# Changing sides between VectorE and GpSimd for 34 two-operand steps, with a new order for the first third

## The chip, the cores and the metric

The kernel runs on one core of a Trainium2 chip. The metric is the device time of one execution in microseconds; the median of three runs of the kernel before is 460.57 (460.49 to 461.0). TensorE (PE) does matrix products, VectorE (DVE) and GpSimd (POOL) do elementwise work, ScalarE (ACT) does activations and copies, SyncE (SP) issues nearly all transfers.

## The reference

A gated linear attention is followed by a two-layer network over its outputs:

```python
f = 1 / (1 + exp(-f_logit))                 # B=4, H=8, S=768, D=48
for t in range(S):
    state = f[:, :, t, :, None] * state + einsum('bhd,bhe->bhde', k[:, :, t], v[:, :, t])
    y[:, :, t] = einsum('bhd,bhde->bhe', q[:, :, t], state)
x = y.transpose(0, 2, 1, 3).reshape(3072, 384)
h = x @ w_in                                # 384 x 2048
out = (h * clip(h + 3, 0, 6) / 6) @ w_out   # 2048 x 384
```

## The kernel before

**Attention.** The sequence is cut into 24 units (4 batches x 6 chunks of 128 positions), numbered chunk by chunk. For unit i: `load`, `loadq`, `loadv` bring gates, q with k, and v (SP); `gate` (ScalarE, line 388) takes the sigmoid; `back` (VectorE scan, 395) makes suffix products, `rend` (411) their reciprocal, `fwd` (419) prefix products, `end` (ScalarE, 414) a copy of the chunk's whole decay. `kmul` (408) and `qmul` (424) multiply k and q by these, on VectorE or GpSimd. TensorE then does `tk` (transpose of k, 482), copied out by `ktok` (ScalarE, 489), `kv` (501), `att` (463), masked by `mask` (VectorE, 470), `qs` (533) and `av` (550); `carry0`, `carry1` (514 to 523) and `decay` (427) hand on the state. `xh`, `xl` (569, 580 or 582) split the result in a high and a low part, and `hole` copies rows within it by DMA; four units make a group of 512 tokens.

**Network.** Each fp32 product is done in three passes of fp32r (high x high, and the two mixed ones). For each of the 16 slices f of the hidden layer the weights come by `ld` and are converted once: `lim` (290 or 292), `z` (298), `mid` (305), `dif` (310), `top` (314) build the word, `high` (ScalarE, 326) the high part, `low` (329, or its halves `lowi`, `lowo`) the low part, on VectorE or GpSimd. For group g and slice f, token number 16g + f: `mm1` (619, nine matmuls), `relu` (ScalarE, 629), `g` (VectorE, 633, reads PSUM), `gh` (ScalarE, 642: high part), `gl` (646: low part, VectorE or GpSimd), `mm2` (669, nine matmuls, the last three of which read gl's result). The first slices of group 0 run in halves (`mm1a`, `relua`, `ga`, `mm2a`, and `...b`; 691 to 710).

**Order.** The program is one list, `ORDER` (line 55), of 1518 tokens `step.index[.banks]`; a loop (998 to 1033) emits them in that order, and each engine executes its own instructions in the list's order (1036 to 1040), waiting where an input or a buffer isn't ready. A step in `ON_POOL` (46) goes to GpSimd, otherwise to VectorE (line 353). SP's transfers stand in the same list, so one that must wait for a free buffer holds up those behind it. `load.i` waits for `qmul.i-2`, `loadq.i` for the last TensorE reader of unit i-3. `warm` and `tiny` are filler matmuls on zeros.

```python
    def engine(op, i):
        return nc.gpsimd if f"{op}.{i}" in ON_POOL else nc.vector
...
    for ins in nc.cur_bb.bb.instructions[begun:]:
        if ins.engine in ORDERED:
            if ins.engine in ordered:
                after(ins, ordered[ins.engine])
            ordered[ins.engine] = ins
```

Of the kernel before, what the change touches and what calls it, by code (L numbers as in the profile page):

```python
# [80 lines left out]
qmul.8 ktok.8 g.14 load.10 att.8.2 g.15 gh.14 kv.8.2 g.16 mm1.17.4 mask.8 rend.9 gl.14 fwd.9 mm2.14 gate.10 gh.15
qmul.9 gl.15 mm2.15 lowo.0 back.10 mm1.19.1 outs.0 outv.1 end.9 gh.16 outs.2 kmul.9 gl.16 relu.17 mm1.18.0 od.2
load.11 rend.10 relu.19 g.17 od.0 decay.8 carry0.8 fwd.10 mm2.16 relu.18 g.19 end.10 carry1.8 g.18 tk.9.3 qmul.10
load.12 mm1.20.4 loadv.10 ktok.9 od.1 gh.17 kmul.10 lowo.1 gh.18 gate.11 decay.9 gl.17 qs.8.0 att.9.2 loadq.11 av.8
kv.9.2 xh.8 carry0.9 mm2.17 gate.12 carry1.9 mask.9 decay.10 lowo.2 back.11 mm1.21.2 gl.18 end.11 gh.19 gl.19 xl.8
tk.10.3 relu.21 mm2.18 ktok.10 g.21 relu.20 rend.11 back.12 qs.9.0 gh.21 fwd.11 att.10.2 loadq.12 av.9 kv.10.0 qmul.11
mm2.19 g.20 load.13 loadv.11 carry0.10 gl.21 loadv.12 carry1.10 rend.12 mm1.22.4 fwd.12 mask.10 mm2.21 relu.22 g.22
kmul.12 decay.11 gh.22 kmul.11 mm1.23.3 gate.13 qmul.12 xh.9 back.13 load.14 hole.8 relu.23 gl.22 mm2.22 xl.9 g.23
hole.9 tk.11.4 qs.10.0 ktok.11 att.11.2 gh.20 loadq.13 av.10 gate.14 gl.20 kv.11.0 loadv.13 tk.12.4 rend.13 mm2.20
ktok.12 gh.23 end.12 gl.23 mask.11 mm1.24.4 decay.12 kmul.13 mm1.25.3 mm2.23 relu.25 relu.24 g.25 g.24 mm1.29.3 gh.24  # L90
gl.24 fwd.13 mm1.26.4 relu.29 gh.25 xh.10 qmul.13 gl.25 mm2.25 load.15 xl.10 relu.26 carry0.11 back.14 mm2.24 g.29
g.26 qs.11.0 gh.26 att.12.2 gl.26 av.11 kv.12.2 xh.11 loadv.14 mm2.26 hole.10 gh.29 carry1.11 mask.12 gate.15
carry0.12 loadq.14 carry1.12 rend.14 mm1.27.4 tk.13.2 relu.27 mm1.30.3 g.27 gl.29 xl.11 mm2.29 relu.30 hole.11 gh.27
g.30 end.13 kmul.14 mm1.28.1 gl.27 gh.30 ktok.13 gl.30 decay.13 back.15 tk.14.0 mm2.30 fwd.14 mm1.31.2 qmul.14 load.16
mm1.32.4 relu.31 relu.28 g.31 end.14 g.28 mm2.27 relu.32 ktok.14 qs.12.0 gh.28 att.13.2 gh.31 loadq.15 gl.28 av.12
g.32 kv.13.2 xh.12 mm2.28 decay.14 gate.16 mask.13 rend.15 carry0.13 carry1.13 fwd.15 mm1.33.4 xl.12 qs.13.2 qmul.15
gl.31 load.17 att.14.0 loadv.15 av.13 kv.14.0 xh.13 mm2.31 relu.33 xl.13 kmul.15 back.16 hole.13 tk.15.2 g.33 end.16
loadq.16 mm1.35.3 ktok.15 hole.12 carry0.14 outv.4 gh.32 end.15 outs.3 gl.32 loadv.16 gate.17 rend.16 mm1.36.2 gh.33
decay.15 fwd.16 outs.5 relu.35 mm2.32 g.35 carry1.14 qmul.16 gl.33 load.18 mm1.34.4 kmul.16 gh.35 back.17 mm2.33
relu.34 relu.36 g.34 g.36 tk.16.3 gl.35 gh.34 mm1.41.4 ktok.16 gl.34 mask.14 qs.14.2 att.15.0 loadq.17 av.14 od.5 od.3  # L100
od.4 kv.15.0 xh.14 mm2.35 xl.14 mask.15 carry0.15 rend.17 mm2.34 decay.16 fwd.17 gh.36 relu.41 g.41 qs.15.0 gh.41
att.16.2 qmul.17 gl.36 av.15 gl.41 kv.16.2 xh.15 mm2.36 gate.18 back.18 mm2.41 carry0.16 rend.18 xl.15 fwd.18 hole.15
mm1.38.4 carry1.16 loadv.17 mask.16 load.19 carry1.15 loadv.18 loadq.18 mm1.40.0 relu.38 mm1.37.3 relu.40 mm1.39.1
relu.37 g.37 g.38 qmul.18 load.20 mm1.44.3 kmul.17 hole.14 gh.38 g.40 gl.38 mm1.43.0 relu.39 gh.40 gl.40 mm2.38 g.39
relu.43 mm2.40 gh.37 end.18 gate.20 gl.37 g.43 mm1.42.1 kmul.18 gh.39 end.17 relu.44 gl.39 g.44 mm2.39 mm2.37 mm1.47.2
gh.44 gh.43 relu.42 gl.43 mm1.46.0 g.42 relu.47 gl.44 g.47 mm2.44 mm2.43 gh.42 gl.42 mm1.51.3 gh.47 relu.46 gl.47
back.20 mm1.45.2 g.46 tk.18.0 relu.45 mm2.42 ktok.18 g.45 relu.51 g.51 tk.17.4 gh.46 mm2.47 ktok.17 gl.46 gate.19
qs.16.0 gh.45 att.17.2 loadq.19 gl.45 av.16 kv.17.0 mask.17 mm2.46 xh.16 decay.18 decay.17 mm1.49.3 mm2.45 relu.49
g.49 carry0.17 xl.16 mm1.48.4 outs.6 back.19 outs.8 gh.51 od.8 od.6 qs.17.0 relu.48 att.18.2 loadq.20 g.48 av.17
# [1048 lines left out]
```

## Time and profile before

| what | us |
|---|---|
| median of three runs | 460.57 |
| profiled execution, first to last instruction | 458.9 |
| TensorE busy | 448.2 |
| VectorE busy | 329.8 |
| ScalarE busy | 225.9 |
| GpSimd busy | 95.0 |

The profile is one execution of the program. Its span goes from the first to the last instruction; a run's time is measured around it. "Busy" is the union of an engine's instructions; the ends of matmuls are modelled. In rows of the trace L408 is line 408 of the kernel, `out<-in` are the program's names for tiles, and `[0.31 <-POOL qkf L408]` says that the engine was idle for 0.31 us before this row and which instruction ended that. The pitch of a full-width matmul (512 columns) is 0.216 us.

### The profile page before, as it was taken

The numbers are of one execution on the slowest core, as the hardware profiler recorded it, in microseconds if no ns is written. First come the engines' busy times: TensorE is split into PE (matmuls) and PEld (weight loads), VectorE is DVE, ScalarE is ACT, GpSimd is POOL, SyncE is SP. The second block draws the span as 40 slices with busy tenths as digits, with TensorE's granted clock in tenths as the row PEclk, the third lists the DMA queues.
The fourth block names the chain that finished last, engine by engine and source line by source line (L and its number), as shares of the span: only waits on it lengthen the run. The fifth ranks groups of instructions, "written<-read, shape, count | busy, mean of one in ns | idle before, by whom it ended". The sixth has DMA issues, their size and how long they took to land.

```text
span 458.9 us, 11919 instructions
## 1 busy us (share of the span) xinstructions
PE 448.2 (98%) x5092; PEld 387.8 (85%) x5092; DVE 329.8 (72%) x538; ACT 225.9 (49%) x390; POOL 95.0 (21%) x110
## 2 busy tenths in 40 slices
...
GB/s 308 270 273 367 413 213 150 99 54 25 182 107 107 23 82 72 123 93 110 84 1 0 102 71 142 62 60 1 70 75 14 14 1 1 23 49 0 1 1 75
DMA packets 19116, 44.95 MB, mean 98 GB/s; under 512 B 2544, under 2 KB 8816, under 8 KB 19056
## 3 DMA queue, kind: packets, MB, share of 16 engines
...
q8 instruction: 42, 0.69, 0.6%
...
q14 instruction: 18, 0.15, 0.1%
...
## 4 chain that ended last, share of the span: by engine, by line
PE 90%; DMA 3%; DVE 3%; issue 1%; ACT 1%; SPq 1%; DVEq 0%; ACTq 0%
PE o L669 33%; PE pair L619 28%; PE single L619 11%; DMA raw<-w 3%; PE pair L533 3%; PE o L833 3%; PE pair L550 2%; PE pair L463 2%; PE single L833 2%; PE pair L833 2%; PE pair L501 2%; PE pair L482 1%; ACT workings L290 0%; DVE workings L314 0%; PE single L482 0%
## 5 line engine op out<-in xcount | busy, mean ns | idle before, releaser
L669 PE MATMUL o<-gg,weight 128*128 128x512 f32 x633 | 148.7, 382 | 0.3 <-issue 0.3
L619 PE MATMUL pair<-xts,weight 128*128 128x512 f32 x594 | 137.6, 381 | 0.0
L669 PEld LDWEIGHTS o<-gg,weight 128*128 128x128 f32 x633 | 117.6, 189 | 16.5 <-issue 0.2
L619 PEld LDWEIGHTS pair<-xts,weight 128*128 128x128 f32 x594 | 110.6, 189 | 15.5 <-DVE tg L633 0.3
L646 DVE TENSOR_TENSOR gg<-tg,gg 128x512 fp32r<-128x512 f32 x76 | 56.2, 746 | 34.4 <-ACT gg L642 34.0
L633 DVE SCALAR_TENSOR_TENSOR tg<-tg,pair 128x512 f32<-128x512 f32 x66 | 44.9, 682 | 41.3 <-ACT tg L629 40.9
L629 ACT ACTIVATE tg<-pair,half 128x512 f32<-128x512 f32 x66 | 44.9, 684 | 59.4 <-PE pair L619 56.7
L642 ACT ACTIVATE gg<-tg 128x512 fp32r<-128x512 f32 x79 | 48.8, 626 | 48.6 <-PE o L669 37.8
L619 PE MATMUL single<-xts,weight 128*128 128x512 f32 x243 | 57.9, 383 | 0.0
L619 PEld LDWEIGHTS single<-xts,weight 128*128 128x128 f32 x243 | 45.2, 189 | 6.6 <-ACT weight L326 0.3
L629 ACT ACTIVATE tg<-single,half 128x512 f32<-128x512 f32 x27 | 18.5, 686 | 31.0 <-PE single L619 28.8
L395 DVE TENSOR_TENSOR_SCAN scans<-scans,ones 112x516 f32<-112x516 f32 (+1 forms) x25 | 30.6, 1229 | 3.8 <-ACT scans L388 3.6
L408 POOL TENSOR_TENSOR qkf<-qkf,scans 112x512 f32<-112x512 f32 x14 | 20.4, 1455 | 59.2 <-DMA qkf<-unit 34.5
L424 POOL TENSOR_TENSOR qkf<-qkf,scans 112x512 f32<-112x512 f32 x11 | 15.8, 1439 | 70.4 <-DVE scans L419 48.7
L419 DVE TENSOR_TENSOR_SCAN scans<-scans,ones 112x516 f32<-112x516 f32 x24 | 29.8, 1240 | 0.4
L569 ACT ACTIVATE xts<-pair 112x512 fp32r<-112x512 f32 x24 | 14.3, 597 | 26.9 <-PE pair L550 22.7
L427 POOL TENSOR_TENSOR carried<-states,ends 112x192 f32<-112x192 f32 x12 | 9.0, 754 | 81.7 <-PE pair L533 48.1
L633 DVE SCALAR_TENSOR_TENSOR tg<-tg,single 128x512 f32<-128x512 f32 x27 | 18.4, 681 | 9.4 <-ACT tg L629 9.4
L470 DVE TENSOR_TENSOR a<-pair,causal 128x512 f32<-128x512 f32 x24 | 16.4, 681 | 8.1 <-PE pair L501 5.3
L582 DVE TENSOR_TENSOR xts<-pair,xts 112x512 fp32r<-112x512 f32 x22 | 15.0, 681 | 8.9 <-ACT xts L569 8.9
L757 POOL TENSOR_TENSOR temporary<-weight 128x256 f32<-128x256 f32 x14 | 10.7, 786 | 44.0 <-DVE tg L633 44.0
L800 ACT ACTIVATE ts<-ts 128x512 fp32r<-128x512 f32 x24 | 14.8, 627 | 9.9 <-DVE ts L796 8.6
...
## 6 DMA issues: line engine op xcount, KB each, us to landing
...
```

The costliest lines, as they stand in the source:

```text
L395: nc.vector.tensor_tensor_scan(flat(sf[:, p])[:, ::-1], gt[:, columns(p)][:, ::-1], flat(unit[:, p])[:, ::-1], 0.0, op0=ALU.mult, op1=ALU.add,
L408: engine("kmul", i).tensor_tensor(parts_of(t, 1), parts_of(t, 1), split(sf[:, :, 1:C + 1]), op=ALU.mult)
L419: nc.vector.tensor_tensor_scan(past, past, flat(rend), 0.0, op0=ALU.mult, op1=ALU.add)
L424: engine("qmul", i).tensor_tensor(parts_of(t, 0), parts_of(t, 0), split(to), op=ALU.mult)
L470: nc.vector.tensor_tensor(d["a"].rearrange("r p e t -> r e p t"), d["at"], causal.unsqueeze(1).unsqueeze(1).broadcast_to([128, 2, NP, HC]) ...
L619: nc.tensor.matmul(h, win(f, a, k), turned(g["xt"][:, k, :g["n"] // C, b]), start=i == 0, stop=i == 3 * KT - 1,)
L629: nc.scalar.activation(d["t"], d["h"], AF.Relu, bias=half, scale=1.0 / 6.0)
L633: nc.vector.scalar_tensor_tensor(d["t"], d["t"], 1.0, d["h"], op0=ALU.min, op1=ALU.mult)
L642: nc.scalar.activation(d["gg"][:, 0], d["t"], AF.Copy)
L646: engine("gl", g["first"] + f).tensor_tensor(d["gg"][:, 1], d["t"], d["gg"][:, 0].bitcast(F32), op=ALU.subtract)
L669: nc.tensor.matmul(g["o"][m], wout(f, a, m), halves_of(g[f]["gg"][:, b]), start=i == 0 and first_in(g, m), stop=f == NF - 1 and i == 2, sk ...
L833: nc.tensor.matmul(place[:, part * 256:(part + 1) * 256], left(a), halves_of(right(b)), start=i == 0 and first_in(g, bank_of), stop=False, ...
```

## The change

`ON_POOL` loses 11 steps, which go to VectorE: decay.5, decay.8, gl.11, gl.14, kmul.8, kmul.9, kmul.12, lowo.0, lowo.2, qmul.13, qmul.15. It gains 23, which go to GpSimd: decay.4, .13, .14; gl.3, .8, .12, .15, .20, .25, .26, .29, .32; kmul.11, .14; low.3, .8, .12, .13; lowo.1; qmul.1, .2, .7, .12. The same 1518 tokens stand in `ORDER`, with the same banks; the first 718 stand in another order, and the last 800 (from about 190 us) as before. No instruction is added or taken away. The core of the diff (lines within the order are cut):

```diff
@@ -44,98 +44,99 @@
 ON_POOL = """
-decay.10 decay.12 decay.15 decay.16 decay.18 decay.19 decay.21 decay.22 decay.5 decay.6 decay.8 decay.9 gl.11 gl.14
-gl.4 kmul.1 kmul.10 kmul.12 kmul.15 kmul.20 kmul.21 kmul.22 kmul.3 kmul.4 kmul.5 kmul.6 kmul.7 kmul.8 kmul.9 low.10
-low.11 lowi.1 lowo.0 lowo.2 qmul.10 qmul.13 qmul.14 qmul.15 qmul.16 qmul.17 qmul.18 qmul.23 qmul.5 qmul.6 qmul.9 se.0
-se.1 se.3 se.4 se.5 se.6 se.7 sl.0 sl.1 sl.3 sl.4 sl.5 sl.6 sl.7 ss.0 ss.1 ss.3 ss.4 ss.5 ss.6 ss.7
+decay.10 decay.12 decay.13 decay.14 decay.15 decay.16 decay.18 decay.19 decay.21 decay.22 decay.4 decay.6 decay.9
+gl.12 gl.15 gl.20 gl.25 gl.26 gl.29 gl.3 gl.32 gl.4 gl.8 kmul.1 kmul.10 kmul.11 kmul.14 kmul.15 kmul.20 kmul.21
+kmul.22 kmul.3 kmul.4 kmul.5 kmul.6 kmul.7 low.10 low.11 low.12 low.13 low.3 low.8 lowi.1 lowo.1 qmul.1 qmul.10
+qmul.12 qmul.14 qmul.16 qmul.17 qmul.18 qmul.2 qmul.23 qmul.5 qmul.6 qmul.7 qmul.9 se.0 se.1 se.3 se.4 se.5 se.6 se.7
+sl.0 sl.1 sl.3 sl.4 sl.5 sl.6 sl.7 ss.0 ss.1 ss.3 ss.4 ss.5 ss.6 ss.7
...
 ORDER = """
-load.0 warm.2 loadq.0 warm.7 tiny.60 load.1 loadv.0 loadv.1 loadq.1 ld.0 gate.0 ld.1 back.0 rend.0 kmul.0 gate.1 fwd.0
-end.0 tk.0.2 tiny.12.3 qmul.0 ktok.0 back.1 load.2 kv.0.0 loadq.2 att.0.0 rend.1 warm.2 warm.1 mask.0 lim.0 kmul.1
-fwd.1 tk.1.4 warm.2 z.0 warm.9 qmul.1 ktok.1 mid.0 load.3 carry1.0 dif.0 carry0.0 gate.2 top.0 qs.0.1 end.1 loadq.3
-av.0 back.2 ld.2 warm.1 xh.0 kv.1.3 lim.1 rend.2 fwd.2 ym.0 att.1.2 warm.5 end.2 xl.0 carry1.1 kmul.2 hole.0 carry0.1
-high.0 qmul.2 tk.2.4 qs.1.1 gate.3 mask.1 loadv.2 loadv.3 mid.1 av.1 back.3 att.2.2 load.4 loadq.4 xh.1 warm.3 z.1
-mask.2 xl.1 ktok.2 rend.3 kmul.3 dif.1 lim.2 hole.1 wd.0 loadv.4 tk.3.0 fwd.3 kv.2.3 ktok.3 carry0.2 mid.2 z.2 kv.3.0
-qmul.3 load.5 qs.2.2 top.1 carry1.3 end.3 carry1.2 att.3.0 dif.2 av.2 high.1 wd.1 ld.3 loadq.5 lowi.0 mm1a.0.4
-carry0.3 top.2 gate.4 xh.2 mask.3 high.2 ym.2 qs.3.0 lowi.1 back.4 relua.0 xl.2 av.3 hole.2 mm1a.1.3 xh.3 lowi.2 end.4
...
-top.5 mm2b.1 relub.2 mid.6 z.6 fwd.5 mm1.4.4 relu.3 dif.6 high.5 gb.2 g.3 gate.6 qs.4.0 qmul.5 low.5 tk.5.2 av.4
-back.6 ktok.5 mm2b.2 loadv.6 xh.4 load.7 top.6 loadq.7 end.6 relu.4 ld.11 kv.5.2 ld.15 g.4 att.5.2 high.6 xl.4 mm1.5.4
...
-dif.10 low.9 tk.7.2 mm1.9.3 ktok.7 top.10 relu.8 fwd.7 high.10 end.7 relu.9 gl.7 mm2.7 g.8 carry0.6 gh.8 g.9 low.10
-mm1.10.4 carry1.6 gh.9 qmul.7 lim.12 mid.11 load.9 gl.8 mm2.8 z.12 hole.5 decay.7 dif.11 mid.12 dif.12 qs.6.2 top.11
-att.7.0 loadq.9 av.6 load.8 top.12 kv.7.0 high.11 relu.10 gl.9 mm2.9 xh.6 carry0.7 mask.7 z.14 g.10 qs.7.0 xl.6 av.7
-low.11 lim.13 z.13 hole.6 mm1.11.2 mid.13 lim.14 xh.7 loadv.9 gh.10 dif.13 high.12 mid.14 gl.10 mm2.10 relu.11 top.13
-gate.8 g.11 low.12 mm1.12.3 gh.11 high.13 carry1.7 xl.7 gl.11 mm2.11 hole.7 relu.12 low.13 z.15 dif.14 loadq.10 gate.9
...
+load.0 warm.2 warm.7 tiny.60 loadq.0 loadv.0 gate.0 loadv.1 warm.2 tiny.12.3 load.1 ld.0 back.0 end.0 loadq.1 ld.1
+rend.0 kmul.0 fwd.0 warm.1 tk.0.2 ktok.0 kv.0.0 qmul.0 gate.1 warm.2 load.2 att.0.0 back.1 warm.9 rend.1 fwd.1 lim.0
+mask.0 z.0 mid.0 kmul.1 tk.1.4 dif.0 loadq.2 carry0.0 ld.2 top.0 qs.0.1 ktok.1 carry1.0 warm.1 qmul.1 load.3 gate.2
+kv.1.3 av.0 loadq.3 att.1.2 xh.0 lim.1 ym.0 end.1 back.2 rend.2 fwd.2 end.2 xl.0 carry0.1 kmul.2 warm.5 high.0 loadv.2
+qs.1.1 mask.1 tk.2.4 qmul.2 gate.3 ld.3 mid.1 carry1.1 av.1 att.2.2 warm.3 hole.0 loadv.3 ktok.2 back.3 xh.1 mask.2
+xl.1 load.4 z.1 loadq.4 kmul.3 rend.3 dif.1 lim.2 kv.2.3 tk.3.0 carry0.2 fwd.3 mid.2 ktok.3 hole.1 loadv.4 z.2 wd.0
+qs.2.2 qmul.3 av.2 kv.3.0 top.1 att.3.0 xh.2 dif.2 load.5 high.1 loadq.5 lowi.0 carry0.3 ym.2 carry1.2 mask.3 carry1.3
+wd.1 gate.4 mm1a.0.4 xl.2 top.2 back.4 qs.3.0 ld.4 av.3 relua.0 ga.0 lowi.1 mm1a.1.3 xh.3 hole.2 xl.3 high.2 relua.1
...
+mm1b.1.0 gb.0 lim.5 mid.5 relub.1 gb.1 dif.5 top.4 low.3 mm2a.2 z.5 mm2b.0 z.6 top.5 high.4 mm1.3.2 lim.6 relub.2
+low.4 mm2b.1 relu.3 fwd.5 mid.6 qmul.5 mm1.4.4 g.3 gb.2 dif.6 ld.11 top.6 tk.5.2 gate.6 back.6 high.5 mm2b.2 ktok.5
+ld.9 qs.4.0 lim.7 kv.5.2 av.4 loadq.7 loadv.6 load.7 gh.3 relu.4 ld.15 g.4 att.5.2 low.5 lim.8 gh.4 xh.4 mm1.5.4
...
+dif.10 low.9 loadq.8 tk.7.2 top.10 mm1.9.3 fwd.7 ktok.7 relu.8 high.10 relu.9 low.10 end.7 g.8 qmul.7 gh.8 g.9 mm2.7
+gh.9 load.9 carry1.6 mid.11 lim.12 dif.11 mid.12 mm1.10.4 z.12 gl.8 xl.5 hole.5 decay.7 mm2.8 dif.12 z.14 qs.6.2
+att.7.0 av.6 top.11 top.12 high.11 kv.7.0 gl.9 lim.13 mm2.9 carry0.7 relu.10 mask.7 xh.6 high.12 xl.6 hole.6 qs.7.0
+low.11 z.13 mid.13 g.10 gh.10 lim.14 dif.13 av.7 low.12 mm1.11.2 loadv.9 top.13 mid.14 xh.7 relu.11 loadq.9 gl.10
+loadq.10 xl.7 mm2.10 high.13 low.13 g.11 carry1.7 gh.11 gate.8 z.15 gl.11 mm1.12.3 mm1.13.4 relu.12 dif.14 top.14
...
```

## Rows read from the trace of the kernel before

**Rows 1.** The page's first part: busy us (share) and instructions of each engine.

```profile
PE 448.2 (98%) x5092; PEld 387.8 (85%) x5092; DVE 329.8 (72%) x538; ACT 225.9 (49%) x390; POOL 95.0 (21%) x110
```

**Rows 2.** Busy time by stretch: start:end, length, then busy us (instructions) per engine.

```profile
0.00:50.00 50.00, 44.42 (x848) 33.72 (x852) 44.09 (x71) 34.20 (x63) 11.34 (x23) 1.00 0.87 314
...
50.00:110.00 60.00, 59.91 (x721) 50.93 (x722) 58.56 (x94) 45.30 (x65) 16.91 (x11) 1.00 0.43 153
...
110.00:459.00 349.00, 343.82 (x3531) 303.19 (x3529) 227.15 (x375) 146.43 (x262) 66.79 (x77) 1.00 0.18 57
```

**Rows 3.** Waits of TensorE: waiter, releaser, us in total, times, longest.

```profile
PE pair L482 <- POOL qkf L408: 0.7, 1, 0.7
...
PE pair L463 <- ACT states L521: 0.4, 1, 0.4
...
PE pair L533 <- ACT carried L514: 0.4, 1, 0.4
...
PE pair L533 <- DVE th L705: 0.4, 1, 0.4
```

**Rows 4.** Timeline to 14 us: start, length, engine, line, operation, [idle before <-releaser].

```profile
4.54 1.66 PE L1014 MATMUL idle<-blank 128*128 128x32 bf16 x60
...
6.31 0.57 PE L482 MATMUL pair<-ident,qkf 112*128 112x112 f32 x4
...
7.40 0.63 ACT L388 ACTIVATE scans<-scans 112x512 f32<-112x512 f32 x1 [3.06 <-DMA scans<-unit]
...
8.04 0.52 ACT L489 ACTIVATE ktok<-pair 128x448 f32<-128x448 f32 x1
...
8.61 0.85 PE L501 MATMUL pair<-v,ktok 64*64 64x48 f32 x46 [1.43 <-ACT ktok L489]
...
9.82 1.19 POOL L408 TENSOR_TENSOR qkf<-qkf,scans 112x512 f32<-112x512 f32 x1 [6.78 <-DMA qkf<-unit]
...
11.07 0.60 PE L482 MATMUL single<-ident,qkf 112*128 112x112 f32 x4 [0.31 <-POOL qkf L408]
...
11.66 1.01 ACT L290 ACTIVATE workings<-raw,topmost 128x768 uint16<-128x768 int16 x1 [3.10 <-DMA raw<-w]
...
11.73 2.32 PE L1007 MATMUL idle<-blank 128*128 128x512 bf16 x10
```

**Rows 5.** Timeline, later places: carry0.1, qs.4, mm1.5.

```profile
18.16 0.33 ACT L514 ACTIVATE carried<-pair 112x192 f32<-112x192 f32 x1
...
48.75 0.65 PE L533 MATMUL pair<-qkf,carried 48*48 48x64 f32 x28 [0.37 <-DVE th L705]
...
52.97 2.21 PE L619 MATMUL single<-xts,weight 128*128 128x512 f32 x9
```

**Rows 6.** Groups by line and shape, VectorE and GpSimd: count, busy us, mean ns.

```profile
L633 DVE SCALAR_TENSOR_TENSOR tg<-tg,pair 128x512 f32<-128x512 f32 x66 | 44.9, 682 | 41.3 <-ACT tg L629 40.9
...
L329 DVE TENSOR_TENSOR weight<-workings,weight 128x768 fp32r<-128x768 f32 x11 | 10.8, 980 | 0.1
...
L310 DVE TENSOR_TENSOR workings<-workings 128x768 int16<-128x768 uint16 x12 | 7.5, 623 | 0.2
...
L408 POOL TENSOR_TENSOR qkf<-qkf,scans 112x512 f32<-112x512 f32 x14 | 20.4, 1455 | 59.2 <-DMA qkf<-unit 34.5 <-DVE scans L395 14.0 <-DMA raw<-w 3.6
...
L646 POOL TENSOR_TENSOR gg<-tg,gg 128x512 fp32r<-128x512 f32 x3 | 3.9, 1283 | 17.6 <-ACT gg L642 15.3 <-DMA v<-unit 2.3
```

**Rows 7.** Timeline from 74 us: low.10, gl.8, mm2.8.

```profile
74.39 2.37 POOL L329 TENSOR_TENSOR weight<-workings,weight 128x768 fp32r<-128x768 f32 x1 [3.63 <-ACT weight L326]
...
77.58 0.69 DVE L646 TENSOR_TENSOR gg<-tg,gg 128x512 fp32r<-128x512 f32 x1
...
77.94 2.11 PE L669 MATMUL o<-gg,weight 128*128 128x512 f32 x9
```

**Rows 8.** Timeline at 35 us: kmul.5 on GpSimd beside dif.3 on VectorE.

```profile
35.37 1.18 POOL L408 TENSOR_TENSOR qkf<-qkf,scans 112x512 f32<-112x512 f32 x1 [3.79 <-DVE scans L395]
...
35.52 1.45 DVE L310 TENSOR_TENSOR workings<-workings 128x768 int16<-128x768 uint16 x1
```

More of the change, by code (lines that the diff above doesn't have):

```diff
@@ L81 @@
[L81 to L109, printed above, removed]
-loadv.19 kv.18.2 outv.7 xh.17 mm1.50.4 se.3 gl.51 gh.48 carry1.17 carry0.18 gl.48 rend.19 mm2.48 fwd.19 relu.50 end.19
@@ new lines @@
+wd.1 gate.4 mm1a.0.4 xl.2 top.2 back.4 qs.3.0 ld.4 av.3 relua.0 ga.0 lowi.1 mm1a.1.3 xh.3 hole.2 xl.3 high.2 relua.1
+wd.2 rend.4 ga.1 hole.3 ld.5 lim.3 lowi.2 mm2a.0 fwd.4 ld.6 kmul.4 end.4 gate.5 tk.4.4 decay.4 mm1a.2.0 z.3 mid.3
+qmul.4 mm2a.1 dif.3 end.3 att.4.2 ktok.4 load.6 back.5 top.3 lim.4 ld.7 relua.2 loadq.6 loadv.5 kv.4.2 end.5 mm1b.0.4
+ga.2 mid.4 mm1b.2.1 carry0.4 ld.8 z.4 ld.14 kmul.5 decay.5 high.3 relub.0 dif.4 carry1.4 ld.10 rend.5 mask.4 loadv.7
+mm1b.1.0 gb.0 lim.5 mid.5 relub.1 gb.1 dif.5 top.4 low.3 mm2a.2 z.5 mm2b.0 z.6 top.5 high.4 mm1.3.2 lim.6 relub.2
@@ new lines @@
+low.4 mm2b.1 relu.3 fwd.5 mid.6 qmul.5 mm1.4.4 g.3 gb.2 dif.6 ld.11 top.6 tk.5.2 gate.6 back.6 high.5 mm2b.2 ktok.5
+ld.9 qs.4.0 lim.7 kv.5.2 av.4 loadq.7 loadv.6 load.7 gh.3 relu.4 ld.15 g.4 att.5.2 low.5 lim.8 gh.4 xh.4 mm1.5.4
+carry0.5 gl.3 gl.4 mm2.3 end.6 kmul.6 mid.7 high.6 mask.5 relu.5 low.6 z.7 ld.12 rend.6 carry1.5 z.8 g.5 dif.7 decay.6
+mm2.4 top.7 gh.5 high.7 mm1.6.4 mid.8 lim.9 dif.8 gl.5 low.7 top.8 z.9 high.8 mid.9 fwd.6 xl.4 relu.6 tk.6.2 mm1.7.3
+ld.13 g.6 lim.10 mm2.5 low.8 relu.7 dif.9 mid.10 gh.6 mm1.8.4 ktok.6 qs.5.0 g.7 top.9 qmul.6 att.6.2 gate.7 hole.4
@@ new lines @@
+loadq.10 xl.7 mm2.10 high.13 low.13 g.11 carry1.7 gh.11 gate.8 z.15 gl.11 mm1.12.3 mm1.13.4 relu.12 dif.14 top.14
+high.14 gate.9 relu.13 back.8 hole.7 low.14 mm2.11 g.13 gh.13 lim.15 mm1.14.1 kmul.8 gl.13 mid.15 mm2.13 rend.8 dif.15
+tk.8.2 top.15 mm1.16.0 high.15 end.8 fwd.8 g.12 gh.12 low.15 relu.14 mm1.15.4 gl.12 qmul.8 g.14 ktok.8 relu.15 back.9
+gh.14 relu.16 att.8.2 g.15 kv.8.2 g.16 mm2.12 mm1.17.4 load.10 gh.15 gl.14 gate.10 lowo.0 mm2.14 gl.15 rend.9 mask.8
+fwd.9 relu.17 mm2.15 mm1.19.1 qmul.9 g.17 decay.8 gh.16 end.9 back.10 outs.0 outv.1 outs.2 kmul.9 gh.17 mm1.18.0
@@ new lines @@
+load.11 rend.10 end.10 carry0.8 od.0 carry1.8 gl.16 fwd.10 qmul.10 load.12 relu.19 relu.18 od.2 tk.9.3 mm2.16 kmul.10
+g.18 g.19 ktok.9 att.9.2 qs.8.0 loadv.10 lowo.1 gh.18 kv.9.2 gate.11 od.1 av.8 loadv.11 gl.17 mm1.20.4 xh.8 gate.12
+mask.9 decay.9 carry0.9 carry1.9 decay.10 mm2.17 gh.19 xl.8 loadq.11 lowo.2 tk.10.3 back.11 gl.18 mm1.21.2 relu.21
+back.12 ktok.10 mm2.18 gl.19 rend.11 g.21 relu.20 gh.21 qs.9.0 att.10.2 loadq.12 av.9 fwd.11 qmul.11 load.13 kv.10.0
+mm2.19 rend.12 carry0.10 g.20 mm1.22.4 loadv.12 carry1.10 gl.21 mm2.21 fwd.12 mask.10 relu.22 g.22 gh.22 gl.22 gate.13
```

90 lines of the change are left out of this document (52 added, 38 removed).

## The prediction

> **What bounds the kernel now.** I read the busy times first: TensorE is busy for 98% of the span, VectorE for 72%, GpSimd for 21% [rows 1]. That is a mean over unlike stages, so the busy times by stretch come next [rows 2]. From 110 us on TensorE leaves about 5 us of 349 idle, nearly all of it the outputs' way home at the very end, and VectorE has a third of its time free: nothing that is reordered there can be worth much. From 50 to 110 us TensorE is idle for 0.1 us of 60, but VectorE is busy for 58.6 of the same 60: TensorE is the bound and VectorE runs level with it. Only in the first 50 us does TensorE stand still, for 5.6 us, of which 1.1 are the start. So the change can gain at most about 4.5 us, all of it before 50 us, and only if VectorE then keeps pace up to 110 us.
>
> The waits of TensorE name the pieces [rows 3]: 0.7 for a product on GpSimd (kmul) and 0.4 each for a state copy, a carry copy and a step of the half-width first stage; the longest, 1.4 for a copy of the transposed keys (ktok), and a 0.3 for kmul stand in the order of time [rows 4]. Around these stand 32 filler matmuls (warm) and 72 tiny ones, as many after as before; a filler moved into a gap is one that does not have to run later, so what counts is idle time alone.
>
> The runs' median is 460.57 us and the profiled span 458.9; the 1.67 us between them lie around the first and last instruction, and I carry them over unchanged. Sums are made on the span.
>
> **The front, wait by wait.** (a) Unit 0. TensorE's tk.0 starts at 6.31, ends near 6.9, and ktok.0 starts only at 8.04, because ScalarE stands in gate.1 (7.40, waiting for the second gate transfer) and end.0; kv.0 starts at 8.61 after 1.43 idle [rows 4]. The new order puts end.0 and ktok.0 ahead of gate.1, and three warm and the twelve tiny matmuls ahead of tk.0. Fillers cost about 0.23 us each (ten in 2.32) [rows 4]; the tiny ones 0.03 (sixty in 1.66). From the end of the sixty at 6.2, with 0.7 and 0.35 of these: tk.0 at 7.25, done 7.85, ktok.0 done 8.4, kv.0 at 8.45. The idle time falls from 1.4 to 0.6: gain 0.8.
>
> (b) Unit 1. loadq.1 goes behind ld.0 on SP's queue. In the trace the arrival of loadq.1 frees kmul.1 at 9.82 and that of ld.0 frees lim.0 at 11.66 [rows 4]: ld.0 costs 1.84 us of transfer, so kmul.1 starts at about 11.7 and, at 1.2 us, tk.1 at 12.9 instead of 11.07. What covers this is filler: from kv.0's start at 8.61 TensorE is busy to 10.76 (tk.1's start less its 0.31 of idle), 2.15 with three fillers in it, so kv.0 and att.0 take 1.45; with eleven fillers (2.55) TensorE is now busy from 8.45 to 12.4 and idle for 0.5 instead of 0.3: loss 0.2. Were kmul.1 later still, nothing covers it. qmul.1, now behind kmul.1 on GpSimd, ends near 14.2 to 15.5; att.1 wants it only at 15.9 behind qs.0, kv.1 and av.0, and load.3, which waits for it on SP with loadq.3, loadv.2 and ld.3 behind, is not wanted before unit 3's gate.3, behind high.0 on ScalarE.
>
> (c) ld.0 lands 1.3 us earlier (512 KB no longer ahead of it), lim.0 and z.0 follow, and carry0.0, which waits behind both on ScalarE, is ready before tk.1 ends: 0.4 gained [rows 3]. (d) qs.1 moves ahead of tk.2 and then waits for carry0.1, which stays at 18.16 to 18.49, since ScalarE's steps from xh.0 to xl.0 stand ahead of it as before [rows 5]; by (a) to (c) TensorE comes there about 1 us earlier than now, near 18.15: loss 0.35. (e) kv.2 goes ahead of tk.3, so kmul.3 and xl.1 are covered: 0.7 gained. (f) att.3 goes behind kv.3 with the carries after high.1: 0.4 gained. (g) mm2b.2 goes ahead of qs.4, which waited at 48.75 for gb.2 to free its bank [rows 5]: 0.4 gained.
>
> Sum of the front: 0.8 - 0.2 + 0.4 - 0.35 + 0.7 + 0.4 + 0.4 = 2.15 us. Its bounds: each of the seven places carries some 0.2 to 0.3 of uncertainty, and the hole transfers before the first half-width product now have ld.3 (another 1.84) ahead in the queue, though ld.2 fills time in which the queue was empty before; I take 1.0 and 2.8.
>
> **The 34 steps.** 23 leave VectorE (nine gl, four low, four qmul, three decay, two kmul, one lowo) and 11 come to it: net 12 instructions, at 0.69 for a gl [rows 7], 0.98 for a low [rows 6] and less for a decay some 9 us less VectorE work in the first 190 us. On GpSimd they take 1.28 (gl), 1.46 (kmul) [rows 6] and 2.37 (low.10) [rows 7], so GpSimd gains some 18 us of work and is still far from full. VectorE's relief buys nothing by itself, since TensorE is the bound; what it buys is that the steps feeding TensorE between 50 and 110 us may be 2 us earlier, which the front's gain needs. By 70 us some 4 us of VectorE work are gone (qmul.1, qmul.2, gl.3 at 0.7, low.3 and low.8 at 1.0), so I cost this at nothing.
>
> What isn't free is what runs longer on GpSimd straight ahead of TensorE. gl.8 ends at 78.27 and mm2.8 starts at 77.94 [rows 7]; only its last three of nine matmuls (at 0.216 us) read gl.8, 1.3 us in, so its margin is 1.0. After the change gl.8 stands on GpSimd behind low.10 (2.37) and qmul.7, and with TensorE 2 us ahead that margin is gone. low.8, low.12 and low.13 go from 0.98 to some 2.37 each. None of these late feeds can be seen in the trace of before, so I bound them: 0, if the earlier start covers all, and 1.4 for each of the three low plus 0.7 for gl.8, 4.9, if none is covered. I take 0.7, one uncovered half-step, nearer to 0 because low.10, on GpSimd before too, made TensorE wait for nothing that the list of its waits names [rows 3].
>
> Forecast: 458.9 - 2.15 + 0.7 = 457.45 of span, **459.1 us** as a run.
>
> **Rivals.** (1) *GpSimd and VectorE stand in each other's way, and the relief is given back.* While kmul.5 ran on GpSimd, dif.3 on VectorE took 1.45 us where that line's mean is 0.62 [rows 6, 8]. But steps that read PSUM, such as g, keep a mean of 0.68 [rows 6]. Eleven more collisions at 0.83 would eat all 9 us. VectorE then comes to 110 us no earlier than before, TensorE waits for it until it has lost the front's gain, and the time is 460.6, between 459.9 and 461.2. The Trainium skill says the same more sharply (page "SBUF — State Buffer", section "Who interferes with whom"): a VectorE instruction with two SBUF inputs and a GpSimd instruction that reads SBUF exclude each other for the whole instruction. By that rule the 18 us that GpSimd gains would be taken from VectorE's two-input steps, twice its relief, and the time would lie at this rival's upper end. The trace agrees on which steps suffer, and shows the loss at one step in so many, not at each.
>
> (2) *Slower: GpSimd's own queue becomes the feeder of TensorE.* low.12 and low.13 stand one behind the other, gl.8 behind low.10 and qmul.7; a late one stops TensorE with everything behind it. It decides from 3 us of such waits on; with the full 4.9, the time is 460.57 - 2.15 + 4.9 = 463.3; half-covered, with a front worth only 1.0, 462. Against it: GpSimd is busy for 17 of the 60 us [rows 2].
>
> (3) *The front is worth all its bound and nothing is late:* 460.57 - 2.8 = 457.8, to 458.4.
>
> (4) *The change does less than it says,* because TensorE's idle time only moves: the 0.2 and 0.35 lost at (b) and (d) are its pattern [rows 4, 5]. With three more such places the front is worth 1.0, and after 0.7 of late feeds the time is 460.3.
>
> **Chances.** Forecast 0.42 (458.4 to 459.6); (3) 0.10; (1) 0.20; (4) 0.11; (2) 0.17. A difference below 0.2%, 0.92 us, can hardly be told from none. Faster: the forecast and (3), 0.52. Same: (1) and (4), 0.31. Slower: (2), 0.17. The range goes from 458.2 to 461.9: it leaves out half of (3) and a good half of (2).
>
> **What would show it.** In the profile after: kv.0 near 8.45 and idle there near 0.6; tk.1 near 12.9; mm1.5 starting near 51 instead of 52.97 [rows 5]; TensorE's idle time before 50 us near 3.6 with the start. If the front is there but the span isn't, the waits of TensorE between 50 and 130 us must name GpSimd lines (gl, low) for rival 2, or VectorE lines with VectorE still full and its two-input steps longer for rival 1. The forecast is wrong if TensorE's waits in the first 50 us still sum to over 4 us.

## The result: 465.77 us, and the profile after

The changed kernel takes 465.77 us (464.96 to 466.79) against 460.53 for the kernel before on the same chip: a ratio of 1.012, with a 95% interval of 1.010 to 1.0141. It is slower by 5.2 us; the forecast was 459.1 and the range ended at 461.9. The profiled execution has a span of 463.9 us, 5.0 above before.

The page's first part, after. It answers [rows 1]:

```profile
PE 448.4 (97%) x5092; PEld 386.8 (83%) x5092; DVE 331.9 (72%) x526; ACT 225.5 (49%) x390; POOL 112.7 (24%) x122
```

TensorE's work is the same to 0.2 us, so all 5 us are idle time. GpSimd gained the foretold 18 us. But VectorE, with 12 instructions fewer, is busy for 331.9 us instead of 329.8: the 9 us taken from it came back, and 2 more. The busy times by stretch, after (columns as in [rows 2]; the last three figures of such a row are the granted share of TensorE's clock, the busy share of the transfer engines and GB/s):

```profile
0.00:50.00 50.00, 43.99 (x814) 33.54 (x815) 44.25 (x69) 34.95 (x65) 17.00 (x26) 1.00 0.92 338
50.00:110.00 60.00, 56.47 (x733) 46.87 (x733) 57.62 (x85) 42.67 (x62) 24.55 (x14) 1.00 0.39 134
110.00:459.00 349.00, 347.92 (x3548) 306.36 (x3546) 229.59 (x374) 147.90 (x264) 71.14 (x82) 1.00 0.18 56
```

Between 50 and 110 us TensorE was idle for 0.1 us before and is now for 3.5, and before 50 us it is idle for 6.0 instead of 5.6. The waits of TensorE, after (columns as in [rows 3]):

```profile
PE o L711 <- DVE th L706: 1.8, 1, 1.8
PE pair L502 <- ACT ktok L490: 1.3, 2, 0.6
...
PE o L670 <- DVE gg L647: 0.9, 1, 0.9
PE pair L483 <- POOL qkf L409: 0.7, 1, 0.7
PE pair L534 <- DVE a L471: 0.6, 1, 0.6
...
PE o L670 <- POOL gg L647: 0.5, 1, 0.5
...
PE pair L620 <- DVE weight L330: 0.4, 1, 0.4
```

Most of the new ones name VectorE (th, gg, a, weight); GpSimd has 1.2 us of them (kmul.7 at 72.22, gl.8 at 81.23). Line numbers are higher by one than before. This is the sign that the prediction named for rival 1: waits for VectorE lines, and VectorE still full.

Where the longest wait comes from is read on the timeline. The stretch that ends in it, after: VectorE, GpSimd and the waiting matmul.

```profile
36.48 1.81 POOL L409 TENSOR_TENSOR qkf<-qkf,scans 112x512 f32<-112x512 f32 x1 [2.29 <-PE pair L502]
...
37.50 1.02 DVE L306 TENSOR_SCALAR workings<-workings 128x768 uint16<-128x768 uint16 x1
38.37 1.83 POOL L330 TENSOR_TENSOR weight<-workings,weight 128x768 fp32r<-128x768 f32 x1
...
38.70 1.71 DVE L428 TENSOR_TENSOR carried<-states,ends 112x192 f32<-112x192 f32 x1
...
41.74 0.40 DVE L706 SCALAR_TENSOR_TENSOR th<-th,single 128x256 f32<-128x256 f32 x1
...
42.20 1.13 PE L711 MATMUL o<-th,weight 128*128 128x256 f32 x4 [1.76 <-DVE th L706]
```

decay.5, which came to VectorE, takes 1.71 us where that form takes 0.35 alone: it ends 0.2 us after low.3, which went to GpSimd. mid.4 (1.02 for 0.34) ends 0.2 us after kmul.5 in the same way. Both stand ahead of gb.0 on VectorE (41.74), which mm2b.0 waits for. The same at 78 us, after:

```profile
78.22 1.31 POOL L425 TENSOR_TENSOR qkf<-qkf,scans 112x512 f32<-112x512 f32 x1
78.51 1.52 DVE L311 TENSOR_TENSOR workings<-workings 128x768 int16<-128x768 uint16 x1
79.49 1.68 POOL L647 TENSOR_TENSOR gg<-tg,gg 128x512 fp32r<-128x512 f32 x1
80.13 1.25 DVE L306 TENSOR_SCALAR workings<-workings 128x768 uint16<-128x768 uint16 x1
...
81.23 0.92 PE L670 MATMUL o<-gg,weight 128*128 128x512 f32 x3 [0.51 <-POOL gg L647]
```

dif.11 ends 0.5 us after qmul.7, mid.12 0.2 us after gl.8; together they lose 1.9 us. The groups by line and shape, after, beside [rows 6]:

```profile
L634 DVE SCALAR_TENSOR_TENSOR tg<-tg,pair 128x512 f32<-128x512 f32 x66 | 44.9, 683 | 44.8 <-ACT tg L630 44.4
...
L647 POOL TENSOR_TENSOR gg<-tg,gg 128x512 fp32r<-128x512 f32 x10 | 15.9, 1594 | 46.9 <-ACT gg L643 46.9
...
L311 DVE TENSOR_TENSOR workings<-workings 128x768 int16<-128x768 uint16 x12 | 8.9, 740 | 0.1
```

g, which reads PSUM, keeps its 683 ns; dif's mean goes from 623 to 740, and gl on GpSimd from 1283 to 1594.

For the rest I use two sums, worked out for every kernel in the same way. *Lengthening*: each VectorE step's time less the time of that shape when nothing is beside it (taken at the end of the shortest quarter of its instances), summed over 36 to 97 us. Before it is 1.0 us, after 9.2; other ways of grouping the shapes give 8.6 to 8.9 after, so the sum is good to some half a microsecond. *Loss*: how much later mm1.14 starts than mm1.4, compared with before; TensorE does the same steps in between in both orders. Before, then after:

```profile
45.84 0.57 PE L619 MATMUL single<-xts,weight 128*128 128x512 f32 x1
...
95.15 1.03 PE L619 MATMUL pair<-xts,weight 128*128 128x512 f32 x4
```

```profile
46.65 0.57 PE L620 MATMUL single<-xts,weight 128*128 128x512 f32 x1
...
99.04 0.38 PE L620 MATMUL pair<-xts,weight 128*128 128x512 f32 x1
```

52.39 us instead of 49.31: a loss of 3.1 us in this stretch. Up to the first matmul of the half-width b part (mm1b.1 at 38.66 before) the changed kernel is 0.68 us ahead; the wait at 42.20 turns that into 0.81 behind; 3.1 us go between 46 and 99, and 0.9 behind that (waits of 0.63 at kv.11 and of 0.35 for a tg at 228).

### The profile page after: what moved, and what is told of

It is laid out like the page before. It is cut to its first block, busy times and chain, and to the rows that moved or that the text cites. A ratio compares the mean times of both kernels' runs of the same rounds, so it can differ in the third digit from the quotient of the medians.

```text
span 463.9 us, 11921 instructions
## 1 busy us (share of the span) xinstructions
PE 448.4 (97%) x5092; PEld 386.8 (83%) x5092; DVE 331.9 (72%) x526; ACT 225.5 (49%) x390; POOL 112.7 (24%) x122
## 4 chain that ended last, share of the span: by engine, by line
PE 80%; DVE 13%; issue 2%; ACT 2%; DMA 1%; SPq 0%; DVEq 0%; ACTq 0%
PE o L670 28%; PE pair L620 26%; PE single L620 10%; PE o L834 3%; PE pair L534 2%; PE single L834 2%; PE pair L834 2%; PE pair L551 2%; DVE scans L396 2%; DVE workings L311 2%; PE pair L464 2%; DVE workings L306 1%; DVE workings L315 1%; DVE tg L634 1%; PE pair L502 1%
## 5 line engine op out<-in xcount | busy, mean ns | idle before, releaser
L647 DVE TENSOR_TENSOR gg<-tg,gg 128x512 fp32r<-128x512 f32 x69 | 52.6, 772 | 28.8 <-ACT gg L643 28.5
L396 DVE TENSOR_TENSOR_SCAN scans<-scans,ones 112x516 f32<-112x516 f32 (+1 forms) x25 | 31.7, 1270 | 5.1 <-ACT scans L389 5.1
L647 POOL TENSOR_TENSOR gg<-tg,gg 128x512 fp32r<-128x512 f32 x10 | 15.9, 1594 | 46.9 <-ACT gg L643 46.9
```

The lines of the kernel that those rows point to most:

```text
L396: nc.vector.tensor_tensor_scan(flat(sf[:, p])[:, ::-1], gt[:, columns(p)][:, ::-1], flat(unit[:, p])[:, ::-1], 0.0, op0=ALU.mult, op1=ALU.add,
L647: engine("gl", g["first"] + f).tensor_tensor(d["gg"][:, 1], d["t"], d["gg"][:, 0].bitcast(F32), op=ALU.subtract)
```

## The experiments

Three theories stand in the expectations. PORT: GpSimd's steps hold up VectorE's steps that work in SBUF, by more than the moved steps relieve it, and VectorE, level with TensorE, passes this on. FEED: what was moved to GpSimd ends late there, straight ahead of TensorE. ORDER: the new list itself puts steps where TensorE waits for them.

**1 and 2. The two halves of the change, one at a time.** The new order with the sides of before; and the old order with the new sides.

```diff
 # e1_order_only                      # e2_sides_only
 ON_POOL = (of before)                +ON_POOL = (of after)
+ORDER   = (of after)                  ORDER   = (of before)
```

> The new order with the sides of before (the same 66 steps on GpSimd). Theory PORT (a GpSimd step and a VectorE step that reads two SBUF tensors, or runs in a fast mode, hold each other up for a whole instruction, and VectorE, level with TensorE from 30 to 100 us, hands the delay on): the collisions of 38 to 95 us go, the time is 459 to 461. Theory FEED (a step that takes 2 us on GpSimd instead of 0.7 to 1.0 comes late to TensorE by its own length, whatever VectorE does): 459 to 461 too. Theory ORDER (the new order itself asks for steps too early): 463.5 or more.

> The order of before with the new sides. PORT and FEED: the 34 changed steps do the harm in any order, 462.5 to 466. ORDER: 460 to 461.

The order alone took 468.17 us (ratio 1.0167, 1.013 to 1.0203), the sides alone 463.53 (1.0053, 1.0031 to 1.0075). For the order alone, PORT and FEED had expected 459 to 461; for the sides alone, ORDER 460 to 461: each missed. Both halves lose, and together they lose less than the order alone: the new order wants the relief that the new sides should bring. The lengthening is some 4.5 us with the order alone and some 7 with the sides alone, so the new sides make VectorE's and GpSimd's steps meet in the old order too. With the sides alone TensorE starts mm1.9 0.97 us ahead of before, loses 1.1 us between mm1.4 and mm1.14 and ends 3.0 us behind; there late feeds can be seen, as FEED has it. The longest of TensorE's waits in that run:

```profile
PE o L670 <- POOL gg L647: 1.6, 2, 1.0
```

**3 and 4. More work on GpSimd and nothing else.** The kernel before, with seven instructions added on GpSimd beside low.3, gl.3, low.8, qmul.7, gl.8, low.12 and low.13, their results unused; once subtractions or a product of two SBUF inputs, once zero-fills of about that length. VectorE still does all its own work.

```diff
+    def beside(step, ...):
+        if step in SHADOWED:
+            nc.gpsimd.tensor_tensor(shadow, x, y, op=ALU.subtract)   # e4_shadow (qmul: mult)
+            nc.gpsimd.memset(shadow[:, :n], 0.0)                     # e5_shadow_memset
     engine(op, f).tensor_tensor(parted(f, 1, cols), src, parted(f, 0, cols).bitcast(F32), ...)
```

> The kernel before, and beside seven steps that the change moved (low.3, gl.3, low.8, qmul.7, gl.8, low.12, low.13) GpSimd does the same two-input work once more into an unused tile, while VectorE still does the real one: no step comes to TensorE from a slower engine, VectorE has its work of before, only GpSimd's reads are added. PORT: VectorE's steps beside them lengthen by 0.3 to 1.2 each, some 4 to 6 us in all, and 1.5 to 4 reach TensorE: 462 to 464.5. FEED: at most GpSimd's own steps behind them are late, 460.4 to 461.5.

> As the run with the added two-input steps, but at the same seven places GpSimd fills the unused tile with zeros for about as long (1280 or 1536 columns, no read of SBUF). PORT, if it is the reading: no VectorE step lengthens, 460.3 to 461.2. If any GpSimd instruction will do, or if what hurts is GpSimd's own queue: as that run.

The reading ones took 467.24 us (1.014, 1.0113 to 1.0167), the fills 459.47 (0.9984, 0.9969 to 0.9999). low.3 on VectorE beside the added subtraction, and beside the added fill:

```profile
39.48 1.82 POOL L333 TENSOR_TENSOR shadow<-workings,weight 128x768 f32<-128x768 f32 x1 [8.33 <-ACT weight L326]
...
40.00 2.11 DVE L337 TENSOR_TENSOR weight<-workings,weight 128x768 fp32r<-128x768 f32 x1
```

```profile
37.55 1.39 POOL L333 MEMSET shadow<- 128x1536 f32 x1 [6.55 <-ACT weight L326]
...
38.08 0.95 DVE L337 TENSOR_TENSOR weight<-workings,weight 128x768 fp32r<-128x768 f32 x1
```

The same step takes 2.11 us in the one and 0.95 in the other. With 467.24 us the subtractions cost more than PORT expected (462 to 464.5). Of the 8.1 us that the profiled execution with subtractions ends behind before, 3.2 are lost before the first added instruction starts (TensorE waits 2.2 us for a ktok at 37.68), which the additions can't explain; the 4.8 behind it are theirs, as far as one execution shows, and none of TensorE's waits there is for GpSimd. The fills, 1.16 to 1.39 us each where the reading steps took 1.28 to 2.89, cost nothing, and low.3 beside one is as fast as alone. So for steps with two inputs it is the reading, not that GpSimd is at work: PORT is shown as a mechanism.

**5. The changed kernel, its moved feeders as fills.**

```diff
+    FILLED = "low.3 low.8 low.12 low.13 gl.3 gl.8 qmul.1 qmul.2 qmul.7".split()
+    def fill(to, behind, more):
+        after(nc.gpsimd.memset(shadow[:, :more], 0.0).ins, made[behind], Sync)
+        after(nc.gpsimd.memset(to, 0.0).ins, made[behind], Sync)
```

> The changed kernel, in which nine of the moved steps of the first 95 us (low.3, low.8, low.12, low.13, gl.3, gl.8, qmul.1, qmul.2, qmul.7) are each replaced on GpSimd by zero-fills of about the same length (1.39 us for 1536 columns, 1.16 for 1280 in the fills measured before), the last of them into the step's own output, waiting for the same input; what these steps compute is left out. Order, VectorE's work and GpSimd's occupancy are those of the changed kernel; only GpSimd's reads of SBUF at these nine places are gone. If the reads take VectorE's time (PORT), some 6 of the 9 us of lengthened VectorE steps before 100 us come back and the kernel runs in 458.5 to 460.5, below the kernel before, near the forecast of 459.1. If late results from GpSimd (FEED) or the order itself (ORDER) cost the time, it stays at 464 to 466.

It took 465.35 us: no gain, against what I expected of PORT. But the lengthening hadn't gone either, it was 8.4 us. The trace says why:

```profile
76.81 2.89 DVE L306 TENSOR_SCALAR workings<-workings 128x768 uint16<-128x768 uint16 x1
77.13 0.75 POOL L333 MEMSET shadow<- 128x768 f32 x1
77.80 0.53 POOL L334 MEMSET qkf<- 112x512 f32 x1
78.28 0.74 POOL L333 MEMSET shadow<- 128x768 f32 x1
78.95 0.53 POOL L334 MEMSET gg<- 128x512 f32 x1
```

mid.11, 0.34 us alone, ends 0.2 us after the last of four fills that stand one behind the other. So a fill does hold up this kind of step; in the run with added fills they had mostly stood beside other kinds.

All traces here together say more. I count the VectorE steps that start while a GpSimd step with two inputs already runs, and are at half of their usual time before it ends; many are the same place in several kernels. Lengthened by over 0.15 us were dif in 21 of 23 cases, qmul in 35 of 35, gl in 89 of 114 and mid in 39 of 51. They then end at a fixed distance behind the GpSimd step: qmul 0.55 us in all 35, dif 0.41 or 0.42 in 19 of 21, mid 0.21 or 0.22 in 35 of 39. So they wait for its end. In the 25 other cases of gl it is the GpSimd step that is long: 1.75 us or more, where the shortest of these steps take 1.19 (a product) and 1.82 (low). Beside a fill, none of 8 two-input steps (gl, dif, qmul) was lengthened, and mid in 2 of 3. Those that read PSUM (g, mask, xl) were lengthened in none of 400.

So this run can't tell the theories apart; runs 8 to 10 can.

**6 and 7. Where in the order it lies.** The new front (171 tokens, to about 36 us) with the old rest, and the old front with the new rest, each with its sides.

```diff
 # e3_front_only                                  # e8_old_front
+ORDER = after[:171] + (before without these)     +ORDER = before[:171] + (after without these)
```

> The new order's first 171 tokens (to about 36 us) with their new sides (qmul.1, qmul.2, decay.4 on GpSimd), then the old order and the old sides. If the loss lies in the collisions behind the front (PORT), the front's own gain is left, about 0.7 to 1 us at 38 us, and the run takes 459.5 to 460.5. If the new front loses by itself (ORDER), it takes 462 or more, with TensorE's long wait near 42 us still there.

> The mirror image: the old order's first 171 tokens with their old sides, then the new order and the new sides. If the loss lies behind 36 us (PORT, and ORDER of the later part), it takes 464 to 466, as the changed kernel does. If the new front is what loses, it takes 461 to 463.

The new front alone took 459.70 us (0.9982, 0.9959 to 1.0005), as fast as before or a little faster, 0.64 us ahead from 52 us on; the old front with the new rest took 466.90 (1.0144, 1.0117 to 1.0171), with a lengthening of 9.0 us. The loss lies behind the front. Nor is the wait at 42.20 the cause of what follows it: the changed kernel with the old sides between 36 and 95 us (the next run) hasn't this wait, starts mm1.4 0.5 us ahead of before and loses 5.4 us from there to mm1.14.

**8 to 10. GpSimd's work between 30 and 97 us taken out.** First the changed kernel with the steps of 36 to 95 us back on their old sides, to part order from sides; then this kernel, the changed one and before with GpSimd quiet.

```diff
 # e6_middle_back: after, with ON_POOL changed
-low.3 low.8 low.12 low.13 gl.3 gl.8 qmul.7
+decay.5 decay.8 gl.11 kmul.8
 # the three quiet kernels, for the steps of 30 to 97 us that are on GpSimd
-    low, gl, decay: tensor_tensor(...)            # two inputs, whole tile
+    low, gl, decay: nc.gpsimd.memset(to, 0.0)     # behind the same ScalarE step
-    kmul, qmul: tensor_tensor(x, x, y)
+    kmul, qmul: tensor_tensor(x[..., :1], x[..., :1], y[..., :1])
```

> The changed kernel with the steps between 36 and 95 us back on the engines they had before (low.3, low.8, low.12, low.13, gl.3, gl.8, qmul.7 on VectorE; decay.5, decay.8, gl.11, kmul.8 on GpSimd); the new order stays, and so do the moved steps of the front and those after 95 us. If collisions alone cost the time (PORT), it comes to 460 to 461. If the new order needs VectorE to be relieved there (ORDER), it loses as the new order with all old sides did, 464 to 468, most of it between 60 and 95 us with TensorE waiting for VectorE lines.

> The kernel before with GpSimd's work between 30 and 97 us left out as far as order and waits allow: low and gl there are only a zero-fill of the step's output (which waits for the same copy on ScalarE), kmul and qmul multiply only the first of the positions along the last axis, decay is a zero-fill. Order, TensorE's and VectorE's work are those of before. Control for the two kernels beside it. In the trace of before VectorE's steps between 36 and 97 us are only 1.0 us longer than alone, so by either theory (PORT or ORDER) it runs in 459 to 460.5.

> The changed kernel with GpSimd's work between 30 and 97 us left out in the same way (low, gl and decay zero-filled, kmul and qmul cut to one position). Order and VectorE's work are those of the changed kernel. PORT: the 9.2 us by which VectorE's steps between 36 and 97 us are lengthened mostly go, VectorE is as much earlier, and the run takes 457.5 to 460. ORDER: TensorE still loses 4 to 5 us between 60 and 95 us because of how the steps are queued, and the run takes 463 to 466.

> The new order with the old sides between 36 and 95 us (466.03 in the run before), with GpSimd's work there left out in the same way. VectorE's own work in this stretch is that of before, and it is not relieved of anything. PORT in its stronger form (the new order is bad only because it brings GpSimd's steps beside VectorE steps that they hold up, 4.9 us more of it than in before): the run takes 459.5 to 461.5. ORDER (the new order needs a relieved VectorE): it stays at 464 to 466.

| order from 36 us | sides, 36 to 95 us | GpSimd | run, us | lengthening | loss |
|---|---|---|---|---|---|
| before | before | works | 460.2 | 1.0 | 0 |
| before | before | quiet | 459.65 | 1.2 | -0.4 |
| after | after | works | 465.77 | 9.2 | 3.1 |
| after | after | quiet | 459.76 | 1.6 | -1.6 |
| after | before | works | 466.03 | 5.9 | 5.4 |
| after | before | quiet | 463.02 | 0.9 | 2.3 |

The kernel before ran in 460.2 to 460.5 us beside these. Lengthening and loss come from one profiled execution each. That of the changed kernel with GpSimd quiet took 462.25 us, above its median: TensorE stood still for 2.03 us at 26.5, waiting for a transfer, and came to mm1.4 2.9 us later than before, which leaves VectorE time to get ahead and makes this loss look small:

```profile
48.71 0.57 PE L637 MATMUL single<-xts,weight 128*128 128x512 f32 x1
```

The busy times from 45 to 95 us (columns as in [rows 2]): the changed kernel, the same with GpSimd quiet, and the new order with the old sides and GpSimd quiet.

```profile
45.00:95.00 50.00, 46.47 (x629) 38.31 (x628) 47.98 (x72) 38.16 (x56) 23.96 (x14) 1.00 0.54 195
```

```profile
45.00:95.00 50.00, 49.84 (x650) 42.69 (x649) 46.69 (x76) 42.05 (x60) 7.28 (x14) 1.00 0.59 216
```

```profile
45.00:95.00 50.00, 46.99 (x632) 38.93 (x631) 47.61 (x78) 39.31 (x57) 4.54 (x9) 1.00 0.54 196
```

The changed kernel with GpSimd quiet runs in 459.76 us (ratio 0.9976, 0.9953 to 1.0): its TensorE is idle for 0.2 us of 50 instead of 3.5. The loss against before is gone. The gain that was forecast isn't there: 459.76 is near 459.1, but the kernel before with GpSimd quiet takes 459.65. Three readings of the table:
- *Sides, without collisions* (fourth and sixth line): worth 2.3 + 1.6 = 3.9 us. By steps it should be four low at 0.98, two gl and a qmul at 0.69, less a decay, a gl and a kmul, 4.3 us, and by the runs it is 463.02 - 459.76 = 3.3. The relief is real.
- *Collisions*: 9.2 - 1.6 = 7.6 us of lengthening cost 4.7 with the new sides, 5.0 cost 3.1 with the old ones: 0.62 of a lost VectorE microsecond reaches TensorE in this stretch, both times, though that the two agree may be luck, given the late start above. By their ratios to before, the runs of these pairs differ by 1.44% and 0.96%, 6.6 and 4.4 us, nearly 0.9 for each microsecond. So 0.6 to 0.9 is an estimate. FEED's part is within this, since a quiet GpSimd is also early, but TensorE's waits for GpSimd are only 1.2 us in the changed kernel, and 0.5 of them for a step that was moved (gl.8).
- *Order, without collisions*: 2.3 + 0.4 = 2.7 us with the old sides, and by the runs 463.02 - 459.65 = 3.4. So by the runs, each good to about 1 us, order and sides cancel (3.4 against 3.3), and what the change loses is the collisions, with the late feeds. VectorE stands waiting for ScalarE in that kernel, most at low.4 (44.76) and low.14 (95.63); both are on VectorE in the changed kernel too, so these waits don't by themselves tell the old sides from the new. Which of them costs the time isn't shown. VectorE's waits from 36 to 97 us there:

```profile
DVE weight L339 <- ACT weight L327: 1.8, 2, 1.1
DVE carried L534 <- ACT xts L587: 1.1, 1, 1.1
DVE workings L306 <- ACT workings L291: 0.8, 1, 0.8
```

So 463.02 fell between what PORT in its stronger form and ORDER expected; both have a part. It is also seen that the new order collides more than the old one even where the sides are the old ones, 5.9 us against 1.0. In the kernel before, low.10 and low.11 ran on GpSimd for 2.37 and 2.20 us without lengthening any VectorE step by 0.1. Beside low.10 stand mainly steps that read PSUM, and one gl, which started in the same moment and kept its time, while low.10 took 2.37:

```profile
74.40 0.67 DVE L646 TENSOR_TENSOR gg<-tg,gg 128x512 fp32r<-128x512 f32 x1
```

Which steps meet is a matter of order and sides together: with its own sides that order has them meet seldom (1.0 us), with the new ones often (some 7).

**11. A version from this.** The new front with one transfer moved, since the front-only kernel waited 0.87 us for hole.3's rows at 37.17.

```diff
-... qs.3.0 ld.4 av.3 ... hole.2 ... hole.3 ld.5
+... qs.3.0 av.3 ... hole.2 ... hole.3 ld.4 ld.5
```

> The kernel with the new front only (the new order's first 171 tokens, then the old order and sides; 459.70 before), with one transfer moved: ld.4 stands behind hole.2 and hole.3 on SP's queue instead of ahead of them, because TensorE waited 0.87 us at 37.17 there for the rows that these move. PORT (nothing collides behind the front: 1 us between 36 and 97 us as in the kernel before, VectorE as loaded as there): the wait goes, the start of mm2b.1 comes to 0.6 to 1.0 us ahead of before's instead of level with it, and the run takes 458.8 to 459.7, 0.2 to 0.4% below the kernel before. ORDER (any new order costs VectorE something behind 50 us): 460.5 or more.

461.65 us (1.0019, 1.0003 to 1.0035), a miss. The wait only changed its name:

```profile
37.87 1.03 ACT L291 ACTIVATE workings<-raw,topmost 128x768 uint16<-128x768 int16 x1 [3.11 <-DMA raw<-w]
38.80 0.47 ACT L701 ACTIVATE th<-pair,half 128x256 f32<-128x256 f32 x1
...
39.30 0.42 DVE L706 SCALAR_TENSOR_TENSOR th<-th,pair 128x256 f32<-128x256 f32 x1 [1.76 <-ACT th L701]
...
39.78 1.27 PE L692 MATMUL pair<-xts,weight 128*128 128x256 f32 x9 [1.37 <-DVE th L706]
```

ScalarE now stands in lim.4 (37.87), waiting 3.1 us for ld.4, with relua.2 behind it; TensorE waits 1.37 for what follows from that. None of the versions is faster than before by more than can be measured, apart from the one with the useless fills, whose interval ends at 0.9999 and of which nothing follows; with GpSimd's work left out, the interval of the changed kernel reaches 1.0.

## Why the prediction was wrong

**The front** was right in its parts and too large in its sum. kv.0's idle time fell to 0.63 (0.6 foretold) and it starts at 8.66 (8.45); tk.1 starts at 12.92 (12.9) after 0.14 of idle (0.5); qs.1 waits 0.19 (0.35). After, from the timeline, with mm1.5 last, which was foretold near 51:

```profile
8.66 0.91 PE L502 MATMUL pair<-v,ktok 64*64 64x48 f32 x48 [0.63 <-ACT ktok L490]
...
12.92 0.60 PE L483 MATMUL single<-ident,qkf 112*128 112x112 f32 x4
...
18.04 0.46 PE L534 MATMUL pair<-qkf,carried 48*64 48x64 f32 x16 [0.19 <-ACT carried L515]
...
52.44 0.92 PE L620 MATMUL single<-xts,weight 128*128 128x512 f32 x3
```

But new waits came where I had none: 0.44 at tk.2 (kmul.2, at 18.94), 0.53 at kv.2 (ktok, held up by z on ScalarE), 0.39 at qs.3. So 0.68 us were won by 38.66 where the terms (a) to (f) gave 1.75, and at 42.20 the collisions took them back. TensorE's idle time before 50 us is 6.0 us with the start of 1.1, not 3.6, and so its waits are over the 4 that the prediction gave as the sign of being wrong. The new waits are rival 4's pattern; by themselves they would have cost 1.1 us of the forecast and kept it in the range, as the front alone shows (459.70).

**The 34 steps** are where it failed: "I cost this at nothing". I took the 9 us less VectorE work as a reserve. Between 36 and 97 us, where 4.3 of it lie, VectorE's remaining steps grew by 8.2 us, so VectorE got later, not earlier, in the stretch where [rows 2] show it level with TensorE (58.6 busy of 60). The quiet kernel shows that with those 8 us, and GpSimd's late feeds, the loss goes (459.76). It doesn't bear out the 2.15 us of the front, as before with GpSimd quiet is as fast (459.65).

**Rival 1** had the mechanism and not the price. The row was there [rows 8], but I read one meeting as a rate ("one step in so many"), and took the rate of an order with few meetings for that of another order with more work on GpSimd. There is no such rate: a step that starts beside a running GpSimd step of the wrong kind mostly waits for the rest of it (dif in 21 of 23 cases, gl in 89 of 114). And I let the loss end when the front's gain was gone, at 461.2. Nothing ends it there: a VectorE that is level with TensorE passes on most of what it loses, an estimated 0.6 to 0.9 of it here. The rule of the Trainium skill (page "SBUF — State Buffer", section "Who interferes with whom") that I set beside it says that the two engines exclude each other for whole instructions, and that a GpSimd step that only writes meets VectorE steps in the fast two-port modes, not those with two SBUF inputs. The traces bear out both (0.95 against 2.11 us for low.3; 2.89 for mid.11). Had I carried 18 us more on GpSimd against 9 us of relief through, it would have given a net loss of up to 9 us of VectorE's time and a rival with the true time in it. The rival's upper end, 461.2, was also no bound: order alone adds to it.

**The late feeds** at 0.7: of the moved steps only gl.8 made TensorE wait, 0.51, and none of low.8, low.12 and low.13. The 0.69 at kmul.7 is another matter: that step was on GpSimd before too, and GpSimd had stood idle for 3.63 us and started 0.14 us after VectorE's back.7, which came 1.7 us later than before. After:

```profile
69.28 1.23 DVE L396 TENSOR_TENSOR_SCAN scans<-scans,ones 112x516 f32<-112x516 f32 x1
...
70.65 1.51 POOL L409 TENSOR_TENSOR qkf<-qkf,scans 112x512 f32<-112x512 f32 x1 [3.63 <-issue]
```

**Rival 2**, the slower one, would have needed 3 us of waits for GpSimd; after the change they are 1.2, and with the sides alone 3.0 (1.6 for gl in two waits, and 1.4 for kmul). The sign came out as rival 2 had it, by another mechanism.

**What no term stood for**: an order is planned for certain durations. With the old sides, and even without collisions, the new list loses 2.7 us between mm1.4 and mm1.14, and the new sides win them back. That its places suit a VectorE that is relieved is my reading of this; the steps that lose the 2.7 aren't singled out.
